# A fused sparse-attention and feed-forward kernel: a new order for the first unit, paired expert steps and casts tied to a stage

## The chip, the core and the metric

The kernel runs on one core of one Trainium2 chip. The metric is the device time of one execution in microseconds (us); before the change it is 223.5 us, the median of 9 runs (222.38 to 225.11). The engines have in-order queues of their own: TensorE (PE: matmuls into PSUM), VectorE (DVE), ScalarE (ACT), GpSimd (POOL) and SyncE (SP, which here only issues DMAs). They wait for one another by semaphores.

## What is computed

The reference takes q, k and v of shape 4 x 8 x 768 x 64 (batch, heads, sequence, head size), in float32, and two weight matrices:

```python
k_sum = k.reshape(B, H, nb, block, D).max(axis=3)      # block = 32, nb = 24
v_sum = v.reshape(B, H, nb, block, D).mean(axis=3)
scores_l = scale * q @ k.T, kept only where |i - j| < 16
scores_s = scale * q @ k_sum.T + log(block)
a = softmax over both kinds of scores together
x = a @ concat(v, v_sum)                               # heads side by side: 3072 x 512
h = x @ w_in                                           # 512 x 2048
g = h * sigmoid(1.702 * h)
out = g @ w_out                                        # 2048 x 512, out is 3072 x 512
```

Each query looks at its neighbours closer than 16 places and at 24 block summaries: the maximum of each block of keys, the mean of each block of values.

## The kernel before, in words

**Units.** The 3072 rows are cut into 8 units of 384 rows: unit `u` is half `u % 2` of batch `u // 2`. A unit's feed-forward part has an input stage and an output stage. The input stage, `ff_in`, makes 16 column tiles of `h`, each from 4 matmuls of 128 x 384 that add up over the four head pairs, and ACT applies the gate to each tile and writes it to `gT`. The output stage, `ff_out`, makes 3 row blocks of 128 rows from 16 matmuls of 128 x 512 each; ACT copies a block to `osb`, and SP sends it out. It is cut into 12 slots of 4 matmuls. In them `beside` puts the attention of the next unit, by the tables `plan`, `plan0` (for unit 1) and `plan1` (for unit 2): `s` are scores of a head pair (PE), their exponential (ACT) and a 0/1 mask product (DVE), `v` the product with the values and the division by the row sums for two head pairs, `x` a PE transpose of the result with a DVE copy, `d` the same by a DMA transpose, `t` the PE transposes of q for batch 1. The result is `xTT[0]` for head pairs 0 and 1 and `xTT[1]` for pairs 2 and 3; the next `ff_in` reads them. For units above 2, `ff_in(u, range(3))` goes through three column tiles at once, first with pairs 0 and 1 and then with pairs 2 and 3, so that the second pair can come later.

**Order by hand.** The wrapper `_Ordered` keeps each engine's instructions in program order. The order written in the code is so the order of each engine's queue, and an instruction that waits holds back all behind it on that engine.

**First unit.** Its attention is written out as a list of small steps, each naming its engine. SP loads k by halves of the sequence, q's first half, v by heads, then q's second half, all for batch 0. `cast_k`, `cast_q`: to bf16. `k_turn`, `q_turn`: transposes on PE. `k_own`, `q_copy`: copies out of PSUM. `k_max`, `k_blocks`, `k_sides`: block maxima, and the neighbour columns of the key tiles. `s_turn`, `s_exp`, `s_mask`: scores, exponential, mask. `b_turn`, `b_exp`: scores of the block maxima. `v_own`, `v_even`, `v_before`, `v_after`: casts of v into the value tiles. `v_sum`, `v_copy`: block sums. `av_near`, `av_blocks`, `v_norm`: values and division. `x_turn`: transposed result. A step is copied by `copy`, in which "dve_alone" stands for a DVE reduction over an axis of length one. `ff_first(p)` then multiplies pair `p` for the first `N0 = 2` column tiles. `warmth(8)` puts 8 wide matmuls on PE at the start, and `idle(n)` puts n small ones, without use for the result, between the steps. They write into spare columns of a PSUM tile that the steps use: `st["idle"]` names that tile.

**Loads of weights.** POOL issues eight loads with a change of type, four quarters of `w_in` and four of `w_out`, in its own queue between its casts. `load_w_in(0)` stands behind `v_own(1, 1, pool)`.

**Later batches.** The k of batch b+2 is loaded by SP in the output stage of an odd unit after slot 0 (`i == 1`), and v and q after slot 7 (`i == 8`). POOL's casts for the next batch are emitted at the beginning of an even unit, but nothing ties them to it: POOL starts on each as soon as its load has landed. `xk` (keys) and `xq` (queries, in the even unit at `i == 10`) are DMA transposes issued by SP; `halo_dmas` and `sum_dmas` fill the neighbour rows and the block rows of the value tiles. `rest_k` makes the block maxima and neighbour columns of the keys in the odd unit. PSUM has two pools: `psb` with 2 tiles of two banks and `pmm` with 4 of one bank.

Of the kernel before, what the change touches and what calls it, by code (L numbers as in the profile page):

```python
# [9 lines left out]
F32 = mybir.dt.float32  # L10
# [24 lines left out]
def kernel(  # L35
# [44 lines left out]

    raw = {}

# [15 lines left out]
    def load_q(b, p, half=None):  # L98
        if half is None:
            t = stage.tile([128, 2, NJ, D], F32, name=f"qf{p}", tag=f"qf{p}0")  # L100
            sp.dma_start(out=t.rearrange("p h j d -> p (h j) d"), in_=chunks(q, b, p))
            raw["q", p] = t
            return
        t = stage.tile([128, 2, JH, D], F32, name=f"qf{p}{half}", tag=f"qf{p}{half}")
        sp.dma_start(out=t.rearrange("p h r d -> p h (r d)"),
                     in_=q[b, 2 * p:2 * p + 2, half * HALF:(half + 1) * HALF]
                     .rearrange("h (p r) d -> p h (r d)", r=JH))
        raw["q", p, half] = t

# [205 lines left out]
    def idle(n):  # L315

        tile, o, start = st["idle"]
        for i in range(n):
            pe.matmul(out=tile[:, o:o + 120], lhsT=warm[:, 0:128], rhs=warm[:, 0:120],
                      start=start, stop=True, skip_group_check=True)  # L320

# [64 lines left out]
    def k_turn(p):  # L386
        src = cast.pop(("k", p))
        big = st["K", p] = psb.tile([128, 1024], F32, name="ps_k", tag="big")
        st["idle"] = big, 904, True
        for half in range(2):  # L390
            for r in range(JH):
                pe.matmul(out=at(big, half * 512 + r, [[JH, 128]]),
                          lhsT=src[:, half, r].rearrange("p h d -> p (h d)"),
                          rhs=ident, start=True, stop=True)
# [25 lines left out]
    def q_turn(p, half=0):  # L420
        src = cast.pop(("q", p))
        if half:
            ps = psb.tile([128, 1024], F32, name="ps_q", tag="big")
        else:
            ps = pmm.tile([128, 512], F32, name="ps_q", tag="mm")
        st["Q", p] = ps
        for r in range(JH):
            pe.matmul(out=ps[:, r * 128:r * 128 + 128],
                      lhsT=src[:, r].rearrange("p h d -> p (h d)"),
                      rhs=ident, start=True, stop=True)  # L430

    def q_copy(p, eng, half=0):

        copy(eng, qT[p][0][:, half * HALF:half * HALF + HALF].rearrange("p (c r) -> p r c", r=JH),
             st["Q", p][:, 0:HALF].rearrange("p (r c) -> p r c", r=JH))

    def s_turn(p):

        big = st["S", p] = psb.tile([128, 1024], F32, name="ps_s", tag="big")
        score_tiles(big, p, 0, 0)  # L440
        st["idle"] = big, 904, True

# [27 lines left out]
    def b_exp(g):  # L470
        ab = st["ab", g] = attp.tile([128, HALF], BF16, name="ab", tag="ab")
        act.activation(out=ab, in_=st["B", g][:, 0:HALF], func=ACT.Exp, scale=scale)

    def v_own(p, hh, eng):
# [24 lines left out]
    def v_copy(p, eng):  # L499
        for hh in range(2):  # L500
            r0 = p % 2 * 64 + hh * 32
            o = p * 128 + hh * D
            copy(eng, vs4[r0:r0 + nb, 2 * p + hh, 0:D], st["VT"][r0:r0 + nb, o:o + D])
        if p == NP - 1:
            st["idle"] = st["VT"], 0, True

# [4 lines left out]
    def av_near(p):  # L511
# [3 lines left out]
        for hh in range(2):  # L515
            for j in range(JH):
                for e in range(2):
# [4 lines left out]
                              start=(hh == 0 and j == 0), stop=False, skip_group_check=True)  # L522
        if p < 2:
            st["idle"] = st["V", p // 2], p % 2 * 512 + 392, False

# [14 lines left out]
    def x_turn(p):  # L540
        src = x_sb.pop(p)
        if p == 0:
            st["X", 0] = pmm.tile([128, 2, HALF], BF16, name="ps_x", tag="mm")
        elif p == 2:
# [121 lines left out]

    N0 = 2
    ph0, seen = [], []
# [38 lines left out]

    gate = consts.tile([128, 2], F32, name="gate")
    dve.memset(gate, 0.0)

# [12 lines left out]
    load_v(0)  # L723
    for p in range(NP):
        load_q(0, p, 1)
    hold = consts.tile([16, 16], BF16, name="hold")
# [5 lines left out]
    cast_k(act, 0, 0)  # L732
    cast_k("dve_alone", 0, 1)
    cast_k(act, 1, 1)
    cast_k(pool, 2, 1)
    cast_k(dve, 1, 0)
    k_turn(0)
    k_own(0, dve)
    cast_k(act, 2, 0)
    idle(5)  # L740
    k_turn(1)
    idle(5)
    k_turn(2)
    k_max(0)
    k_own(1, act)
    k_sides(0, dve)
    cast_k(act, 3, 0)
    k_own(2, act)
    k_blocks(0, pool)
    cast_k(dve, 3, 1)  # L750
    k_sides(1, pool)
    k_sides(2, pool)
    k_max(1)
    cast_q(pool, 2, 0)
    cast_q(act, 0, 0)
    idle(4)
    k_turn(3)
    cast_q("dve_alone", 1, 0)
    k_max(2)
    idle(2)  # L760
    q_turn(0)
    k_own(3, act)
    k_sides(3, dve)
    k_blocks(1, pool)
    q_turn(1)
    q_copy(0, act)
    cast_q(pool, 3, 0)
    q_copy(1, act)
    q_turn(2)
    k_blocks(2, pool)  # L770
    idle(3)
    b_turn(0)
    v_own(0, 0, act)
    s_turn(0)
    s_turn(1)
    v_before(0, pool)
    k_max(3)
    v_own(0, 1, "dve_alone")
    b_turn(1)
    q_copy(2, dve)  # L780
    s_exp(0)
    s_exp(1)
    v_even(0, pool)
    q_turn(3)
    b_exp(0)
    v_sum(0)
    s_mask(0, dve)
    s_mask(1, dve)
    v_own(1, 0, act)
    q_copy(3, dve)  # L790
    v_own(2, 0, "dve_alone")
    v_own(1, 1, pool)
    s_turn(2)
    idle(10)
    v_sum(1)
    load_w_in(0)
    v_own(2, 1, "dve_alone")
    s_exp(2)
    s_turn(3)
    k_blocks(3, pool)  # L800
    idle(3)
    b_turn(2)
    v_after(0, act)
    b_turn(3)
    av_near(0)
    v_copy(1, dve)
    v_before(2, pool)
    v_before(1, "dve_alone")
    v_even(2, act)
    v_sum(2)  # L810
    v_copy(0, dve)
    v_own(3, 1, "dve_alone")
    v_copy(2, dve)
    v_own(3, 0, pool)
    v_even(1, act)
    v_after(1, act)
    s_exp(3)
    load_w_in(1)
    idle(6)
    av_blocks(0, 0, D + 1)  # L820
    av_near(1)
    v_after(2, act)
    v_sum(3)
    b_exp(1)
    av_blocks(1, 0, D + 1)
    s_mask(2, dve)
    s_mask(3, dve)
    v_even(3, pool)
    av_near(2)
    v_norm(0)  # L830
    av_blocks(2, 0, D + 1)
    v_after(3, act)
    v_copy(3, act)
    v_before(3, pool)
    idle(7)
    x_turn(0)
    v_norm(1)
    av_near(3)
    av_blocks(3, 0, D + 1)
    v_norm(2)  # L840
    idle(2)
    x_turn(1)
    gelu_soon()
    copy(act, xT[0], st["X", 0 // 2][:, 0 % 2])
    copy(act, xT[1], st["X", 1 // 2][:, 1 % 2])
    idle(8)
    ff_first(0)
    idle(2)
    x_turn(2)
    v_norm(3)  # L850
    copy(dve, xT[2], st["X", 2 // 2][:, 2 % 2])
    idle(6)
    x_turn(3)
    copy(dve, xT[3], st["X", 3 // 2][:, 3 % 2])
    ff_first(1)
    ff_first(2)
    ff_first(3)
    load_w_in(2)
    load_w_in(3)
    for c in range(4):  # L860
# [8 lines left out]
    for p in range(NP):  # L869
# [6 lines left out]
    plan1 = {0: ["t0"], 1: ["t1"], 2: ["s0", "s1"], 4: ["t2"], 5: ["t3"],  # L876
             6: ["v0", "s2", "s3", "d0"], 9: ["v1"], 11: ["x1"]}

# [4 lines left out]
    def beside(u, slot):  # L883
        b, half = u // 2, u % 2
        for what in (plan0 if u == 1 else plan1 if u == 2 else plan).get(slot, ()):
# [11 lines left out]
            else:  # L897
                tx(i)

    for u in range(2 * B):  # L900
        b, half = u // 2, u % 2
        todo = {}
        if u == 0:
            for p in range(NP):
                cast_q(dve, p, 1)
                todo[4 + p] = [lambda p=p: (q_turn(p, 1), q_copy(p, dve, 1))]
        elif u == 1:
# [13 lines left out]
        elif half == 0 and b + 1 < B:  # L921
            s = (b + 1) % 2
            for p in range(NP):
                cast_k(pool, p)
                if p % 2:
                    xk(p // 2, s)
            for p in range(NP):
                cast_v(pool, s, p, 0)
                cast_v(pool, s, p, 1)
            for p in range(NP):  # L930
                cast_q(pool, p)
        elif b + 1 < B:
            s = (b + 1) % 2
            todo = {1: [lambda: rest_k(0, s)], 3: [lambda: rest_k(1, s)],
                    6: [lambda: rest_k(2, s)], 8: [lambda: rest_k(3, s)]}
        if u == 1:
            for p in range(NP):
                clear_kx(pool, p, 0)
            clear_vw(pool, 0)
        if u > 2:  # L940
            ff_in(u, range(3))
        for nt in range(0 if u else N0, NT):
            if u <= 2 or nt > 2:
                ff_in(u, (nt,))
# [10 lines left out]
        for ms, part in order:  # L955
# [16 lines left out]
            elif half and b + 2 < B and i == 1:  # L972
                for p in range(NP):
                    load_k(b + 2, p)
            elif half and b + 2 < B and i == 8:
                load_v(b + 2)
                for p in range(NP):
                    load_q(b + 2, p)
            elif half == 0 and 0 < b < B - 1 and i == 10:
                s = (b + 1) % 2  # L980
                vsum(s, range(NJ))
                block_sums()
                xq(0, s)
                xq(1, s)
                w5 = vw[s].rearrange("p (j e) h c -> p j e h c", e=2)
# [32 lines left out]
```

## Time and profile before

| | |
|---|---|
| median of 9 runs | 223.5 us (222.38 to 225.11) |
| the profiled execution: its time, its span | 222.64 us, 220.9 us |
| first expert matmul (`ph`) | 24.31 us into the span |
| first unit's output stage begins | 36.70 us |
| input stages of units 1 to 7 begin | 50.83, 78.73, 102.89, 126.34, 150.56, 173.62, 196.68 us |
| last output copied | 217.58 us |
| DMA, mean over the span | 169 GB/s |
| read from and written to HBM | 27.26 MB, 6.29 MB |

A stage begins where the chain of waits passes from one kind of expert matmul to the other. In the rows of the profile, PE is the matmuls and PEld the loading of their weights; `ph` is the PSUM tile of the input stage, `po` of the output stage, `ps_s` of scores, `ps_av` of values, `ps_k` and `ps_q` of transposed k and q. A row of a timeline has start, length, engine, line, operation, output and inputs, the shape, how many in a row, and in brackets how long the engine was idle before and who released it. As all instructions go through one wrapper, their line is 27.

### The profile page before, as it was taken

What the parts mean: (1) busy time and instruction counts of PE and PEld (TensorE: products, weight loads), DVE (VectorE), ACT (ScalarE), POOL (GpSimd) and SP (SyncE); (2) the same over time, 40 slices, a digit from 0 to 9 for tenths busy, and PEclk for the clock granted to TensorE, in tenths of its full rate; (3) what the DMA queues carried; (4) which work ended last, traced back from release to release, by engine and by line L of the source; (5) the groups of instructions that cost most, each with busy time, mean ns of one, the idle gap of its engine ahead of it and who ended that gap; (6) DMA issues with size and microseconds to landing.
All of it is one profiled execution on the core that took longest, in us unless ns stands there. A gap on an engine that the chain in (4) does not pass through costs nothing.

```text
span 220.9 us, 5025 instructions
## 1 busy us (share of the span) xinstructions
PE 209.4 (95%) x1989; PEld 118.3 (54%) x1989; DVE 92.0 (42%) x262; ACT 136.9 (62%) x241; POOL 67.2 (30%) x164
## 2 busy tenths in 40 slices
PE   7588999999999999999999999999999999999993
PEld 3456665556554556454655465445654564556542
DVE  5789780545985710376408100649026001700000
ACT  3688568465677657862788277735786478637420
POOL 5377983044954438410004166400000000000000
PEclk9999999999999999999999999999999999999999
DMA  5999999999999999999999999999703300340012
GB/s 169 315 218 235 212 211 217 165 230 214 254 314 195 224 236 218 239 148 179 173 193 235 200 225 215 204 157 217 157 14 98 119 0 3 83 131 2 0 47 96
DMA packets 94408, 37.36 MB, mean 169 GB/s; under 512 B 78705, under 2 KB 91441, under 8 KB 94385
## 3 DMA queue, kind: packets, MB, share of 16 engines
q1 hardware_dynamic: 90160, 32.85, 73.7%
q0 software_dynamic: 4224, 4.19, 11.5%
q8 instruction: 15, 0.25, 0.5%
q14 instruction: 9, 0.07, 0.1%
HBM read 27.26 MB, written 6.29 MB: 152 GB/s over the span
## 4 chain that ended last, share of the span: by engine, by line
PE 76%; DMA 8%; DVE 6%; SPq 4%; ACT 2%; issue 2%; POOL 0%; DVEq 0%; ACTq 0%; POOLq 0%
PE ph L27 36%; PE po L27 32%; DMA w_in_sb<-in_moe_w_in_dram 4%; SPq L27 4%; PE ps_av L27 3%; PE ps_s L27 2%; DMA vf<-in_v_dram 2%; DMA xT<-x 2%; DVE a_sb L27 2%; ACT a_sb L27 1%; DVE kx L27 1%; PE ps_q L27 1%; DVE ks L27 1%; DVE qT L27 1%; PE ps_vs L27 1%
## 5 line engine op out<-in xcount | busy, mean ns | idle before, releaser
L27 PE MATMUL po<-w_out_sb,gT 128*128 128x512 bf16 (+2 forms) x400 | 89.0, 371 | 0.0
L27 PE MATMUL ph<-xT,w_in_sb 128*128 128x384 bf16 x512 | 86.3, 326 | 1.0 <-DMA xT<-x 0.4
L27 ACT ACTIVATE gT<-ph 128x384 bf16<-128x384 f32 x128 | 61.6, 491 | 27.4 <-PE ph L27 27.2
L27 PEld LDWEIGHTS <-w_in_sb 128*128 128x128 bf16 x512 | 49.4, 98 | 33.8 <-issue 1.0
L27 PEld LDWEIGHTS <-gT 128*128 128x128 bf16 x400 | 36.4, 98 | 38.5
L27 DVE TENSOR_TENSOR a_sb<-a_sb,mk 128x768 bf16<-128x768 bf16 x32 | 19.4, 620 | 75.1 <-ACT a_sb L27 73.9
L27 ACT ACTIVATE osb<-po 128x512 f32<-128x512 f32 (+1 forms) x24 | 14.2, 592 | 36.8 <-PE po L27 36.7
L27 ACT ACTIVATE a_sb<-ps_s 128x768 bf16<-128x768 f32 x32 | 24.3, 806 | 7.6 <-PE ps_s L27 7.6
L27 POOL CAST vw<-vf 128x768 bf16<-128x768 f32 (+3 forms) x35 | 24.2, 720 | 14.4 <-DMA vf<-in_v_dram 13.9
L27 POOL CAST kb<-kf 128x768 bf16<-128x768 f32 (+1 forms) x13 | 11.0, 848 | 47.1 <-DMA kf<-in_k_dram 47.1
L27 ACT ACT_TABLE_LOAD x16 | 20.5, 1283 | 1.1 <-PEq L1002 0.8
L27 DVE TENSOR_TENSOR x<-ps_av,rc 128x384 bf16<-128x384 f32 x28 | 15.6, 557 | 1.0
L27 POOL CAST qb<-qf 128x384 bf16<-128x384 f32 (+1 forms) x18 | 11.4, 651 | 9.1 <-DMA qf<-in_q_dram 6.0
L27 PEld LDWEIGHTS <-a_sb 128*64 128x64 bf16 x384 | 8.1, 111 | 7.3 <-DVE a_sb L27 3.6
L27 DVE TENSOR_REDUCE ks<-kx 128x24 bf16<-128x768 bf16 x12 | 11.2, 937 | 0.3 <-ACT kx L27 0.3
L27 PE MATMUL ps_av<-vw,a_sb 128*64 128x65 bf16 x384 | 10.3, 198 | 0.6 <-DVE a_sb L27 0.4
L27 DVE COPY osb<-po 128x128 f32<-128x128 f32 x1 | 0.3, 292 | 24.9 <-PE po L27 24.9
L27 DVE COPY kx<-kx 128x80 bf16<-128x80 bf16 (+4 forms) x52 | 9.6, 237 | 0.9 <-ACT kx L27 0.9
L27 PE MATMUL ps_s<-qT,kx 64*128 64x64 bf16 x384 | 9.2, 191 | 0.5 <-DVE qT L27 0.2
L27 PEld LDWEIGHTS <-kx 64*128 64x128 bf16 x384 | 7.0, 95 | 4.8 <-issue 3.9
L27 PEld LDWEIGHTS <-warm 128*128 128x128 bf16 x71 | 5.4, 107 | 6.8 <-issue 5.2
L27 DVE RECIPROCAL rc<-ps_av 128x6 f32<-128x6 f32 x32 | 6.0, 188 | 6.6 <-PE ps_av L27 6.6
(70 smaller groups left out, 118.1 us busy)
## 6 DMA issues: line engine op xcount, KB each, us to landing
out_dram<-osb SPq DMA_DIRECT2D x23, 256.0 KB, 2.3
kf<-in_k_dram SPq DMA_DIRECT2D x12, 384.0 KB, 6.2
vf<-in_v_dram SPq DMA_DIRECT2D x12, 384.0 KB, 6.4
qf<-in_q_dram SPq DMA_DIRECT2D x16, 192.0 KB, 4.2
qf<-in_q_dram SPq DMA_DIRECT2D x8, 384.0 KB, 6.3
w_in_sb<-in_moe_w_in_dram POOLq DMA_DIRECT2D x4, 512.0 KB, 9.5
w_out_sb<-in_moe_w_out_dram POOLq DMA_DIRECT2D x4, 512.0 KB, 16.6
kf<-in_k_dram SPq DMA_DIRECT2D x8, 192.0 KB, 3.5
```

Source lines behind the costliest of these rows:

```text
L27: r = f(*a, **kw)
```

## The change

- **First unit.** The list of steps is rewritten: other orders and other engines for many steps. `load_w_in(0)` now stands behind `v_own(1, 0, pool)` and `k_sides(3, pool)`.
- `q_turn` writes its three transposes with a step of 3 in PSUM for the first half, and `q_copy` then copies a plain run.
- **Idle matmuls.** `idle` does nothing until a bank is named. It is the bank of q's last turn, once that is copied out, then that of the second block scores, once their exponential is taken. 34 idle matmuls are asked for instead of 63; each is 128 wide instead of 120.
- **Late q.** The second half of q of batch 0 is one load of all heads, issued by POOL between the third and the last quarter of `w_in`, instead of four loads by SP after v. Its turns in unit 0 come after column tiles 11 to 14, instead of 4 to 7.
- `N0` is 3: `ff_first` multiplies three column tiles.
- **Pairs.** `ff_in(u, range(3))` is used for units 1 and 2 also. For unit 2, the first two head pairs are transposed by PE (`x0` at slot 8) and no longer by DMA (`d0` at slot 6).
- **Casts.** From unit 2 on, POOL copies one element of the unit's first gate output to `gate2` before its casts, so that they can't begin earlier. k and v are cast in an even unit, q in the odd unit after it. q is loaded in the even unit after the key transposes, and `xq` is issued in the odd unit behind the casts of q. v is loaded after slot 6 instead of slot 7.

The core of the diff (in the list of the first unit only the start and the end, and the loads):

```diff
     def load_q(b, p, half=None):
...
+        if half and p == 0:
+            late[0] = stage.tile([128, NP, 2, JH, D], F32, name="qfl", tag="qfl")
+            if b == 0:
+                pool.dma_start(out=late[0].rearrange("p i h r d -> p (i h) (r d)"),
+                               in_=q[0, :, HALF:S].rearrange("h (p r) d -> p h (r d)", r=JH))
...
     def idle(n):
-        tile, o, start = st["idle"]
+        if st.get("idle") is None:
+            return
         for i in range(n):
-            pe.matmul(out=tile[:, o:o + 120], lhsT=warm[:, 0:128], rhs=warm[:, 0:120],
-                      start=start, stop=True, skip_group_check=True)
+            pe.matmul(out=st["idle"][:, 0:128], lhsT=warm[:, 0:128], rhs=warm[:, 0:128],
+                      start=True, stop=True)
...
     def q_turn(p, half=0):
-            pe.matmul(out=ps[:, r * 128:r * 128 + 128],
+            pe.matmul(out=ps[:, r * 128:r * 128 + 128] if half else at(ps, r, [[JH, 128]]),
...
     def q_copy(p, eng, half=0):
+        if half == 0:
+            copy(eng, qT[p][0][:, 0:HALF], st["Q", p][:, 0:HALF])
+            if p == NP - 1:
+                st["idle"] = st["Q", p]
+            return
...
     def b_exp(g):
+        if g:
+            st["idle"] = st["B", g]
...
-    N0 = 2
+    N0 = 3
...
     cast_k(act, 0, 0)
-    cast_k("dve_alone", 0, 1)
-    cast_k(act, 1, 1)
+    cast_k(pool, 2, 0)
+    cast_k(dve, 0, 1)
+    k_turn(0)
     cast_k(pool, 2, 1)
+    k_own(0, act)
     cast_k(dve, 1, 0)
-    k_turn(0)
-    k_own(0, dve)
-    cast_k(act, 2, 0)
+    cast_k(dve, 1, 1)
+    k_turn(1)
+    k_own(1, act)
+    cast_k(act, 3, 0)
+    k_turn(2)
+    k_own(2, act)
+    cast_q(act, 0, 0)
+    k_sides(0, pool)
+    cast_k(pool, 3, 1)
+    k_turn(3)
...
+    v_own(1, 0, pool)
+    s_mask(2, dve)
+    v_sum(0)
+    v_own(1, 1, act)
+    k_sides(3, pool)
...
+    load_w_in(0)
+    v_own(2, 0, pool)
...
+    av_blocks(3, 0, D + 1)
     ff_first(0)
+    v_norm(2)
     x_turn(2)
+    copy(act, xT[2], st["X", 2 // 2][:, 2 % 2])
     v_norm(3)
+    ff_first(1)
     x_turn(3)
     copy(dve, xT[3], st["X", 3 // 2][:, 3 % 2])
     ff_first(2)
     ff_first(3)
     load_w_in(2)
+    for p in range(NP):
+        load_q(0, p, 1)
     load_w_in(3)
...
-             6: ["v0", "s2", "s3", "d0"], 9: ["v1"], 11: ["x1"]}
+             6: ["v0", "s2", "s3"], 8: ["x0"], 9: ["v1"], 11: ["x1"]}
...
+    def pool_after(u):
+        pool.tensor_copy(out=gate2, in_=gT[u % 2][:, 0, 0:1])
+
+    def turn_keys(u, b):
+        s = b % 2
+        pool_after(u)
+        for p in range(NP):
+            cast_k(pool, p)
+            if p % 2:
+                xk(p // 2, s)
+        for p in range(NP):
+            load_q(b, p)
+        for p in range(NP):
+            cast_v(pool, s, p, 0)
+            cast_v(pool, s, p, 1)
+
+    def turn_queries(u, s):
+        pool_after(u)
+        for p in range(NP):
+            cast_q(pool, p)
+            if p % 2:
+                xq(p // 2, s)
...
-                todo[4 + p] = [lambda p=p: (q_turn(p, 1), q_copy(p, dve, 1))]
+                todo[11 + p] = [lambda p=p: (q_turn(p, 1), q_copy(p, dve, 1))]
...
         elif half == 0 and b + 1 < B:
+            todo = {0: [lambda: turn_keys(u, b + 1)]}
         elif b + 1 < B:
             s = (b + 1) % 2
-            todo = {1: [lambda: rest_k(0, s)], 3: [lambda: rest_k(1, s)],
+            todo = {0: [lambda: turn_queries(u, s)],
+                    1: [lambda: rest_k(0, s)], 3: [lambda: rest_k(1, s)],
                     6: [lambda: rest_k(2, s)], 8: [lambda: rest_k(3, s)]}
...
-        if u > 2:
+        if u:
             ff_in(u, range(3))
...
-            elif half and b + 2 < B and i == 8:
+            elif half and b + 2 < B and i == 7:
                 load_v(b + 2)
-                for p in range(NP):
-                    load_q(b + 2, p)
             elif half == 0 and 0 < b < B - 1 and i == 10:
                 s = (b + 1) % 2
                 vsum(s, range(NJ))
                 block_sums()
-                xq(0, s)
-                xq(1, s)
```

## The prediction

> **What bounds the kernel now.** I read the engine sums first, then a table of stages, the chain of waits, and single engines in order of time. Part 1 of the page says that TensorE is the bound:
>
> ```profile
> PE 209.4 (95%) x1989; PEld 118.3 (54%) x1989; DVE 92.0 (42%) x262; ACT 136.9 (62%) x241; POOL 67.2 (30%) x164
> ```
>
> Only 11.5 us of the span have no matmul. The stage table says where (columns: stretch, its length, PE busy, then PEld, DVE, ACT, POOL, clock, DMA share, GB/s):
>
> ```profile
> 5.00:10.00 5.00, 3.14 (x28) 2.70 (x27) 3.48 (x7) 2.47 (x5) 1.42 (x5) 1.00 1.05 325
> 20.00:24.30 4.30, 3.45 (x66) 2.70 (x62) 3.72 (x11) 3.25 (x8) 4.28 (x7) 1.00 1.19 234
> 25.90:36.70 10.80, 10.80 (x75) 6.61 (x74) 6.44 (x25) 7.20 (x15) 8.23 (x45) 1.00 1.22 215
> 36.70:50.80 14.10, 13.80 (x159) 7.01 (x157) 6.08 (x14) 8.28 (x12) 2.88 (x3) 1.00 1.15 201
> 89.30:102.90 13.60, 13.48 (x170) 6.41 (x168) 7.47 (x17) 7.57 (x11) 2.49 (x3) 1.00 1.11 181
> 136.80:150.50 13.70, 13.29 (x169) 6.59 (x168) 7.29 (x17) 7.55 (x11) 3.32 (x4) 1.00 1.03 192
> 184.00:196.70 12.70, 12.70 (x147) 6.27 (x145) 4.96 (x12) 7.57 (x11) 0.00 (x0) 1.00 0.29 75
> ```
>
> From 25.9 us on PE has hardly a gap: a unit's input stage is 64 matmuls in 10.4 us, its output stage 48 wide ones (10.3 us) and the next unit's attention. An undisturbed output stage lasts 12.66 us (184.02 to 196.68 in the chain), or 13.11 with the 0.45 us of block sums (ps_vs). So there are two places to gain: the start, and the excess of some stages. At the start the chain of waits (start, length, what) reads:
>
> ```profile
> 14.89 0.50 POOL vw L27
> 15.39 0.04 issue
> 15.43 8.83 DMA w_in_sb<-in_moe_w_in_dram
> 24.26 0.05 issue
> 24.31 0.50 PE ph L27 x2
> ```
>
> The first expert matmul starts when w_in's first quarter lands, and that load waits in POOL's queue for a cast of v. Two of the unit's 64 input matmuls (0.163 us each) are done when the others begin at 25.86, an effective start at 25.5. The loads that follow are close behind (issue to landing of the w_in quarters, then w_out's):
>
> ```profile
> DMA to landing us min/median/max: 8.8/9.5/11.9
> DMA to landing us min/median/max: 13.9/16.6/19.3
> ```
>
> Asked issue by issue, with the issues at 15.43, 17.97, 20.37, 21.10 and 21.84, w_in lands at 24.26, 27.4, 30.0, 33.0 and w_out's first quarter at 35.7. They are first used at 24.3, 28.1, 31.4, 34.1 and 36.7 (0.65 us a column tile, 0.17 a q turn): the last two have only 1 us of slack.
>
> **The change: first unit.** Loads of k, q, v keep their order, so their landings stand: k halves 3.46 to 8.72 (waits of the casts), q 9.5 to 11.1 (issue plus 4.6), v at 14.77, 17.5 and 19.43 for the fourth, seventh and eighth half (waits of POOL), the others set between at 0.9 us. With the rows of before (ACT 0.52 and DVE 0.36 for a half cast, 0.81 for k_own on ACT, 0.95 for k_max, 0.82 for a turn of k, 0.62 a mask, 0.76 a norm) I walked the new order through the in-order queues. Before, the fill matmuls sat in the bank being read, and the turn behind them waited:
>
> ```profile
> 7.19 0.42 PE L27 MATMUL ps_k<-warm 128*128 128x120 bf16 x5 [1.05 <-DVE kx L27]
> 8.37 0.82 PE L27 MATMUL ps_k<-ident,kb 128*128 128x128 bf16 x6
> 11.51 0.67 PE L27 MATMUL ps_q<-ident,qb 128*128 128x128 bf16 x9
> ```
>
> After: k turns start at 4.7, 6.55 (cast of the half that lands at 6.12), 7.96, 9.29, against 4.66, 7.45, 8.37, 10.75; q turns at 10.1 to 11.1; s_turn(0) at 11.6 instead of 13.54. Then v's landings rule. v_sum(0) comes at 13.5 (second half 12.8, cast 0.5). ACT takes v_own(1,1) at 14.8, v_copy(0), v_even(1) and b_exp(0), so av_blocks(0) starts at 16.6 (19.41 before) and av_near(1) at 17.7. The last half of v is cast by 19.85 on DVE and 20.45 on ACT (v_even, v_after): v_sum(3) at 19.9, v_copy(3) to 20.9, av_near(3) 21.2, av_blocks(3) to 21.9, last norm to 22.7. On POOL the load of w_in's first quarter stands behind v_own(1,0) (lands 13.8, ends 14.3) and k_sides(3) (0.6): issue 14.9 instead of 15.43. The late q loads, 0.77 MB beside it before, are now behind w_in's third quarter. Quarters follow each other in 2.6 to 3.1 us, so the first lands at 22.0: 2.3 us earlier. ff_first(0) holds x_turn(2), x_turn(3) and two xT copies behind it, 22.05 to 24.6, with 12 matmuls in place of 8: effective start 22.7, 2.8 us earlier.
>
> This gain is clipped. The stream then runs 22.0, 24.7, 27.3, late q (2.0 to 2.6 us at 0.3 to 0.38 MB/us), w_in's last quarter 32.4, w_out's first 35.1. PE would want the last quarter at 30.6 and waits 1.8 us (minus a q turn). Four column tiles of 0.65 and three q turns of 0.17 end the stage at 35.5 where it was 36.7. **First term: 1.2 to 1.4, taken as 1.3 us.** The DVE casts of late q, first in DVE's queue behind xT and keys (26.3), now wait to 29.9; behind them are only the q copies (0.8 each), wanted at 35.4 or later, and masks wanted at 37.9. POOL ends its constant masks about 1 us later, 34.6, still in time. The software load of 1024 rows has no row; the w_in issue of 512 rows takes 0.74 to 0.88, so I take 0.9 to 1.7 on POOL, hidden behind a full queue.
>
> A rule against it: the Trainium skill, "PSUM — Partial Sum Buffer", Specifications, says that any non-contiguous access pattern slows matmuls significantly, and q's turns now write with step 3. The rows agree and size it: six strided k turns take 0.82, nine plain ones 0.67, so about 0.10 against 0.057 each: 0.15 us a turn on PE. By the rule alone this is a loss of 0.6; but q_copy reads plain and falls from 0.80 to about 0.5 (k_own's 0.96 for twice the width), which stands on the way to s_turn(0). I count nothing net, as v rules afterwards (bounds −0.3 to +0.6). A second: "TensorE: Matmul & The Clock Gate", in its table for kernels, allows no PE gaps over about 3 us; from its window of 3.4 us I estimate up to 1.7 us lost at half rate. Here 63 fills become 34, none before 14.3 us. The row shows clock 1.00 at 3.14 us busy of 5; the walk has turns and scores for about 6.5 of the 9.6 us after 4.7, gaps under 0.8. So by the row nothing; the rule's 1.7 stays in the range.
>
> **Three column tiles by pairs.** In unit 1 PE waited 0.32 us for the DVE copy of the second pair (50.2 to 50.8). Three tiles give 6 matmuls, 0.98 us, on the first pair. Gain 0.3 (0 if a PSUM bank comes late). In unit 2 it waited 0.37 for the DMA transpose. That becomes 6 PE transposes (0.34) and a DVE copy (0.56) at slot 8; the gap from 78.20 to 78.73 goes. Net 0.15; bounds −0.3 (a PSUM bank more, held for 1 us) to 0.4. In unit 1 the 0.27 us wait of a k turn for DVE also goes, since with an earlier start the first key chain ends before POOL's v casts.
>
> **Casts held to input stages.** Rows where POOL's casts meet DVE:
>
> ```profile
> 92.04 0.83 POOL L27 CAST qb<-qf 128x768 bf16<-128x768 f32 x1 [1.01 <-DMA qf<-in_q_dram]
> 92.08 1.66 DVE L27 TENSOR_TENSOR a_sb<-a_sb,mk 128x768 bf16<-128x768 bf16 x2 [13.12 <-ACT a_sb L27]
> 139.52 1.91 DVE L27 TENSOR_TENSOR a_sb<-a_sb,mk 128x768 bf16<-128x768 bf16 x2 [17.41 <-ACT a_sb L27]
> ```
>
> A free pair of masks lasts 1.26. The losses are 0.40, 0.65 and, at 119.22 (1.40), 0.14; the output stages of those units are 13.57, 13.80 and 12.89 long, 0.46, 0.69 and 0.23 over their base. So the masks are the excess. After, 4 k and 8 v casts at 0.83 start at the first gelu, 1.9 us into the input stage, and end at 11.9; masks come at 13.3. Free: 1.2 us (bounds 0 to 1.4). In odd units POOL's four q casts (1.9 to 5.3) meet the key copies, which stretch from 0.36 to about 1.2 as at 54.32; DVE has until 13, so nothing. xq, behind halos and sums on SP, is issued 3.6 to 7.0 into the unit and lands 4.1 later, first needed at 10.5: covered by 2 us, each us beyond would be paid. v's loads go one slot earlier, ahead of an output that then waits some 5 us on SP (76.94 to 81.96 before); it has three buffers, so nothing. q's loads leave that place and stand behind the key transposes (a rival below).
>
> **Sum.** 1.3 + 0.3 + 0.27 + 0.15 + 1.2 = 3.2 us. The profiled execution took 222.64 (span 220.9 and 1.7 around it), the lower end of the runs; it becomes 219.4. Against the median of 223.5: 220.3.
>
> **Rivals.** *Weights don't clip* (0.16): the first load starts sooner than its issue tells, or late q passes quickly; then the first term is 2.8 and the time 218.8. For it: the stream shared with late q before. Against: the same bytes before w_in's last quarter.
> *The stream starts as before* (0.20): v's last half and the software queue set its start, so the last quarter lands at 33.0; first term 36.7 − 36.1 = 0.6, the masks give half, 0.6, and the small terms lose 0.2. 1.0 in all: 222.5, own range 221.5 to 224.4.
> *SP's queue turns slower than before* (0.20): in units 2 and 4 the key transposes now wait on POOL and have q's loads, an output and both x transposes behind them. Counted from the unit's start: first pair cast at 3.6, four transposes 6.8 (10.4), four loads 7.1 (17.5), output 1.7, x transposes 3.4: 22.6. Before they ended at 23.4 and PE did not wait. A slip beyond 0.8 us is paid in both units; it eats 3.2 at 2.4 us and passes 0.5% at 3. If transposes beside v's loads cost 3.5, 225.7.
>
> **Chances.** A measurement can tell about 0.5%, 1.1 us. The forecast (219.3 to 221.5) has 0.44. Faster: 0.44 + 0.16 + 0.05 of the second rival; same: 0.15, and 0.01 of the last; slower 0.19. The range 218.2 to 224.6 leaves out 0.04 below, 0.16 above.
>
> **To look for.** Right: the first ph matmul near 22, a PE wait on w_in near 31, mask pairs near 1.26 everywhere, output stages of 13.1 and 12.7. Wrong: clock under 1.00 in the first slices, ph waiting on DMA xT at units 3 and 5, ps_s on DMA qT, or a first ph after 23.

## The result, and the profile after

The kernel after takes **221.33 us** (median of 16 runs, 220.46 to 222.43) against 223.06 for the kernel before on the same chips (53 runs): ratio 0.9925, 95% interval 0.9906 to 0.9945. That is 1.7 us faster, inside the range and in the direction forecast, but half of the 3.2 us that the sum gave. The profiled execution took 220.88 us, its span is 219.1 us. Some executions of a kernel fall into a slower state; the ratios leave those out and the medians do not, so where the two differ the ratio counts.

The same rows as before the change, first the engine sums of the page:

```profile
PE 209.2 (95%) x1966; PEld 116.4 (53%) x1966; DVE 93.4 (43%) x261; ACT 136.7 (62%) x243; POOL 69.2 (32%) x169
```

PE's work is the same; what it does not work has gone from 11.5 to 9.9 us. The stage table (stretch, length, PE busy, then PEld, DVE, ACT, POOL, clock, DMA share, GB/s), with the edges set to this kernel's stages:

```profile
5.00:10.00 5.00, 4.12 (x26) 2.11 (x25) 3.67 (x9) 3.49 (x6) 2.89 (x8) 1.00 1.06 332
20.00:23.00 3.00, 3.00 (x62) 2.51 (x60) 1.58 (x4) 1.60 (x4) 3.00 (x4) 1.00 1.23 197
25.20:37.30 12.10, 10.38 (x73) 6.31 (x71) 7.11 (x25) 7.03 (x15) 9.29 (x48) 1.00 1.19 244
37.30:50.80 13.50, 13.50 (x159) 6.92 (x157) 5.88 (x14) 7.83 (x12) 1.65 (x2) 1.00 1.09 188
89.00:102.20 13.20, 13.20 (x169) 6.46 (x168) 6.53 (x17) 7.61 (x12) 1.17 (x2) 1.00 1.04 199
135.70:148.90 13.20, 13.20 (x170) 6.50 (x169) 6.55 (x17) 7.58 (x12) 1.21 (x2) 1.00 1.26 219
```

The output stages of units 2 and 4 are as forecast: 13.2 us and full. The first input stage (third row) has 1.7 us without a matmul where there was none. PE's row and the chain of waits show for what:

```profile
34.20 0.82 PE L27 MATMUL ph<-xT,w_in_sb 128*128 128x384 bf16 x4 [1.69 <-DMA w_in_sb<-in_moe_w_in_dram]
```

```profile
13.84 0.51 POOL vw L27
14.36 1.54 POOL kx L27 x2
15.89 0.05 issue
15.94 0.32 PE ps_s L27 x10
...
20.00 0.69 POOL w_in_sb L27
20.68 0.88 POOL qfl L27
21.57 12.59 DMA w_in_sb<-in_moe_w_in_dram
34.15 0.04 issue
34.20 0.82 PE ph L27 x4
```

The last quarter of w_in is issued at 21.57 and lands at 34.15. Stage by stage (starts of the first matmul of each kind, from PE's rows in order of time), the difference between the two profiled executions is:

| | before | after | difference |
|---|---|---|---|
| first `ph` | 24.31 | 23.03 | −1.28 |
| unit 0, input stage | 12.23 | 14.28 | +2.05 |
| unit 1, input and output stage | 13.21, 15.50 | 12.41, 15.40 | −0.90 |
| output stages of units 2, 3, 4 | 13.75, 12.89, 13.82 | 13.22, 12.66, 13.22 | −1.36 |

(Unit 0's output stage is the same to 0.01, and so are the stages from unit 5 on. The span is 0.3 us shorter than these rows add up to; that lies behind the start of the last input stage.) The first unit costs 0.77 us here, where 1.3 of gain was forecast; pairs and casts give somewhat more than was forecast.

### The profile page after: what moved, and what is told of

Read it like the earlier page. It is cut to its first block, busy times and chain, and to the rows that moved or that the text cites. A ratio compares the mean times of both kernels' runs of the same rounds, so it can differ in the third digit from the quotient of the medians.

```text
span 219.1 us, 4973 instructions
## 1 busy us (share of the span) xinstructions
PE 209.2 (95%) x1966; PEld 116.4 (53%) x1966; DVE 93.4 (43%) x261; ACT 136.7 (62%) x243; POOL 69.2 (32%) x169
## 2 busy tenths in 40 slices
DMA packets 92711, 37.15 MB, mean 170 GB/s; under 512 B 77857, under 2 KB 89569, under 8 KB 92689
## 4 chain that ended last, share of the span: by engine, by line
PE 84%; DMA 10%; POOL 2%; SPq 1%; DVE 1%; issue 0%; DVEq 0%
PE po L27 39%; PE ph L27 35%; DMA w_in_sb<-in_moe_w_in_dram 6%; PE ps_av L27 4%; PE ps_s L27 3%; DMA vf<-in_v_dram 3%; DMA kf<-in_k_dram 2%; PE ps_q L27 1%; SPq L27 1%; POOL vw L27 1%; POOL kx L27 1%; DVE qT L27 1%; PE ps_t L27 1%; PE ps_vs L27 1%; PE ps_x L27 1%; PE ps_vt L27 0%
## 5 line engine op out<-in xcount | busy, mean ns | idle before, releaser
L27 ACT ACTIVATE gT<-ph 128x384 bf16<-128x384 f32 x128 | 60.9, 491 | 26.9 <-PE ph L27 26.8
L27 DVE TENSOR_TENSOR a_sb<-a_sb,mk 128x768 bf16<-128x768 bf16 x32 | 17.6, 555 | 65.8 <-ACT a_sb L27 64.5
L27 ACT ACTIVATE osb<-po 128x512 f32<-128x512 f32 (+1 forms) x24 | 14.2, 592 | 37.0 <-PE po L27 36.8
L27 ACT ACTIVATE a_sb<-ps_s 128x768 bf16<-128x768 f32 x32 | 24.2, 805 | 6.7 <-PE ps_s L27 6.7
L27 POOL CAST vw<-vf 128x768 bf16<-128x768 f32 (+3 forms) x36 | 25.0, 749 | 3.2 <-DMA vf<-in_v_dram 2.9
L27 POOL COPY gate<-gT 128x1 bf16<-128x1 bf16 x4 | 0.8, 191 | 60.4 <-ACT gT L27 60.4
L27 DVE COPY kx<-kx 128x80 bf16<-128x80 bf16 (+4 forms) x48 | 12.6, 315 | 0.0
L27 PE MATMUL ps_av<-vw,a_sb 128*64 128x65 bf16 x384 | 9.8, 198 | 0.8 <-DVE x_sb L27 0.8
L27 DVE CAST qT<-ps_q 128x384 bf16<-128x384 f32 (+1 forms) x8 | 7.2, 900 | 4.9 <-PE ps_q L27 4.8
```

What stands on the lines that cost most here:

```text
L27: r = f(*a, **kw)
```

## Where the weights lose their lead

Issues and landings of the loads show the lead going. w_in's quarters and w_out's first land at 24.26, 27.4, 30.0, 33.0, 35.7 before, and at 21.4, 24.2, 28.7, 34.15, 37.05 after, with late q at 30.9 between. The first quarter is 2.8 us earlier, the last 1.15 later. The window from 16 to 18 us before, then the windows after (columns as above):

```profile
16.00:18.00 2.00, 1.67 (x39) 1.23 (x37) 1.97 (x5) 2.00 (x5) 1.62 (x6) 1.00 1.13 249
```

```profile
14.00:16.00 2.00, 0.86 (x10) 0.33 (x11) 1.96 (x5) 1.54 (x5) 2.00 (x4) 1.00 1.24 216
16.00:18.00 2.00, 2.00 (x43) 1.61 (x44) 1.25 (x4) 1.99 (x6) 1.94 (x4) 1.00 0.59 109
18.00:20.00 2.00, 1.23 (x27) 0.98 (x25) 1.57 (x4) 1.45 (x4) 1.90 (x5) 1.00 1.15 188
20.00:22.00 2.00, 2.00 (x40) 1.66 (x38) 1.22 (x3) 0.64 (x2) 2.00 (x3) 1.00 1.23 192
22.00:24.00 2.00, 1.69 (x30) 1.08 (x26) 1.09 (x4) 1.92 (x5) 2.00 (x4) 1.00 1.10 162
```

In 16 to 18 us the DMA engines are half empty: share 0.59, 109 GB/s, where before it was 1.13 and 249. In quarters of a microsecond the share is 0.13 to 0.20 from 17.0 to 18.0 and back at 1.08 from 18.25. SP has issued its last load of v at 14.7 us; before, four late q loads followed it and ran on beside the first weights. After, nothing follows, and the first load from POOL's queue, issued at 15.83, moves hardly a byte until 18.0. It was no quicker before: issued at 15.43, it moved its first packets at 17.9, but the late q filled the time. So the stream of weights does not start sooner; its first load has the engines for itself and lands sooner. At 24.26, when the first quarter lands before, POOL's queue has moved 0.92 MB there, nearly two quarters, and the late q is all but done: 5.70 MB since the start, against 5.13 after. From 14 to 30 us 3.53 MB moved before and 3.30 after (the dip at 22 to 24 is made up by 353 GB/s at 26 to 28): 0.23 MB less, 1.1 us at 0.21 MB/us, the lateness of the last quarter. **My theory A**: the late q load, moved to POOL's queue, leaves DMA time unused, and all that comes behind the first weights pays. Rivals: POOL's queue issues too late; the place of late q in the stream; fewer idle matmuls (clock).

## The experiments

**Late q by SP again**, the rest as after; `load_q` issues each load on SP. Ratios here and below are to the kernel before, with 95% intervals.

```diff
+    for p in range(NP):
+        load_q(0, p, 1)          # four loads by SP, behind load_v(0)
...
-    for p in range(NP):          # one load by POOL, behind load_w_in(2)
-        load_q(0, p, 1)
```

> The changed kernel with late q loaded as before, by four loads of SP right behind v. Theory A (the DMA engines ran empty for about 1.2 us between the end of v and the first weights, since nothing was queued behind v): the share of the DMA in 16 to 18 us goes from 0.59 back to over 1.1, w_in's first quarter lands later (23.5 to 24.3) but the last one at 32.3 to 33.0 instead of 34.15, PE's wait for it falls under 0.5 us, and the time is 0.6 to 1.5 us below the changed kernel. Theory B (late q in front of w_in's last quarter costs its own 2.3 us, no time is lost on the engines): the first quarter still lands by 22 and the last by 31.9, and PE doesn't wait; 1.7 us below. Theory C (the late start is what the wait hides, so a later first matmul gives all back): within 0.3 us of the changed kernel.

219.68 us (6 runs), ratio 0.9847 (0.9805 to 0.9889): 1.65 us below after. The window in question and PE's wait for w_in, from this run:

```profile
16.00:18.00 2.00, 2.00 (x42) 1.61 (x43) 1.42 (x5) 1.99 (x6) 1.94 (x4) 1.00 1.02 189
27.52 5.37 PE L27 MATMUL ph<-xT,w_in_sb 128*128 128x384 bf16 x32 [0.59 <-DMA w_in_sb<-in_moe_w_in_dram]
```

PE waits 0.6 us for w_in (its second quarter) instead of 1.7 (its last), w_in's last quarter lands at 32.66, w_out's first at 35.8, and the output stage begins at 36.00. With 12 idle matmuls instead of 3 ahead of the last scores on top of that:

> The kernel with late q by SP, with 12 idle matmuls instead of 3 in front of the scores of the fourth head pair, where PE is busy 0.84 of 2 us (14 to 16 us). Theory A: the clock keeps at 1.000 in all executions, and the median is within 0.3 us of the kernel with 3, or below where that one lost the clock. Theory B (fills delay the scores behind them): 0.3 to 0.6 us above.

219.86 us, 0.9859 (0.9814 to 0.9903), its output stage from 36.29: the same. These two are the fastest versions of the study, below both kernels. The second one limits theory A, though. Its window is nearly as empty as that of after, as SP issued the last late q only at 18.14:

```profile
16.00:18.00 2.00, 1.87 (x34) 1.31 (x34) 1.50 (x4) 1.96 (x6) 2.00 (x5) 1.00 0.67 131
```

Yet w_in's last quarter lands at 32.5, and w_out's first at 36.25, half a microsecond behind the version with the full window. So these 2 us are not the whole of what late q by SP gives.

**The first weight load earlier**, behind `v_own(0, 1, pool)`, in the kernel after and in the version above.

```diff
     v_own(0, 1, pool)
+    load_w_in(0)
...
-    load_w_in(0)
     v_own(2, 0, pool)
```

> The changed kernel with the load of w_in's first quarter issued one cast and one copy step earlier in POOL's queue, right behind the casts of the first head pair of v (about 13.4 us instead of 15.8). Theory A (the DMA engines run empty between v and the first weights): the weights start while v still loads, the share of the DMA in 16 to 18 us rises from 0.59 to over 1.0, w_in's last quarter lands at 32.6 to 33.4 instead of 34.15, PE's wait of 1.7 us halves, v's last half and with it the first expert matmul come up to 1 us later; 0.5 to 1.2 us below the changed kernel. Theory B (late q in front of the last quarter costs its own length): the whole stream moves by the 2.4 us, the last quarter lands at 31.8, the wait goes; 1.7 us below.

> Both: late q by SP behind v, and the first quarter of w_in issued at 13.4 us. Theory A: with late q behind v the engines have hardly any empty time left (shares of 1.02 to 1.26 between 14 and 22 us), so the earlier issue only lets the weights take their turns from v; the last quarter lands within 0.5 us of 32.7, v's last half later, and the time is within 0.5 us of the kernel with late q by SP alone. Theory B: the stream moves by its 2.4 us again, 0.6 us below that kernel, as its rest of wait goes.

222.44 us, 0.9973 (0.9942 to 1.0005): not below after but 1.1 above, so this expectation fell. The first issue was at 13.50 and the window 16 to 18 was full (1.21), but 20 to 22 was emptier instead (0.80): the third quarter, behind POOL's later casts of v, was issued at 22.04 instead of 19.94, and PE waited 1.1 us for w_out. The hole moved. (In 5 of the 12 executions, the profiled one among them, the mean granted clock was 0.992, too; the other 7 have a median of 222.28, so the clock alone is not the cause.) With late q by SP the same move gives 220.16, 0.9871 (0.9829 to 0.9914), within 0.5 us of the version it was made from. So an earlier first issue is not what was lacking; that it was something to move meanwhile fits both runs.

**Late q behind w_in's last quarter**, its four turns after column tile 15.

```diff
     load_w_in(2)
-    for p in range(NP):
-        load_q(0, p, 1)
     load_w_in(3)
+    for p in range(NP):
+        load_q(0, p, 1)
```

> The kernel after, with the load of late q behind w_in's last quarter instead of ahead of it, and its four turns all after column tile 15. Theory A (the first stage is late because the DMA engines run nearly empty between v's end and the first weights; all that lies behind is late by it, in whatever order): w_in's last quarter lands near 31.8 us and PE does not wait for it, but w_out's first quarter still lands near 37, and the output stage of unit 0 begins at 36.8 to 37.4 us: time 220.8 to 221.8, within 0.5 us of the kernel after. Theory B (the place of late q between the quarters costs the 1.7 us that PE waits for the last quarter): the output stage begins near 35.7, 1.2 to 1.7 us below the kernel after, 219.6 to 220.2.

221.34 us, 0.9928 (0.9901 to 0.9955): exactly after. PE no longer waits for w_in, but w_out's first quarter lands at 37.4, and late q at 34.5, with casts and copies of DVE behind it (PE waits 2.0 us for these), so that the output stage begins at 37.97, 0.6 later than w_out would have allowed. Theory A holds for the total: w_out's first quarter comes no sooner in either order, and that order chooses only who waits. The kernel may owe part of its time to the late copies, so that this run alone would not settle it.

**A tiny load first** in POOL's queue, near the start.

```diff
     masks0()
+    early = consts.tile([16, 16], BF16, name="early")
+    pool.dma_start(out=early, in_=moe_w_in[0:16, 0:16])
```

> The kernel after, with one tiny load added in POOL's queue near the start of the kernel (16 x 16 elements of w_in to a tile that nobody reads), so that the first weight load is not the first transfer of that queue. The question is to what the 2.2 us belong in which the DMA engines are half empty before w_in's first bytes. Theory A (to the first use of the queue): w_in's first quarter lands 1 to 2 us sooner than 21.4 us, DMA share from 16 to 18 us near 1.0 instead of 0.59, the last quarter near 33.0, and the time 0.8 to 1.3 us below the kernel after. Theory B (to every load of this kind[...]): landings and share as in the kernel after, time within 0.4 us of it.

220.90 us, 0.9901 (0.9870 to 0.9932), 0.4 below after by the medians and 0.5 by the ratios, which the intervals don't tell apart. The first quarter needs 5.7 us from issue to landing (5.6 after) and the last lands at 33.9 (34.15); so the delay is not the queue's first use. Theory B.

**No idle matmuls** in the first unit (all 34 left out).

```diff
-    idle(3)                      # and the eight others
     s_turn(3)
```

> The changed kernel without any of the 34 idle matmuls of the first unit (the 8 wide ones at the start stay). Theory A (the clock is cut when PE does too little for some 3 us, as in 16 to 19.5 us of one execution of the first unit alone): the granted clock falls in most executions, to a mean of 0.985 to 0.992, the first expert matmul comes 0.5 to 1.5 us later, and the time is 0 to 1.0 us above the changed kernel (the wait for the last quarter of w_in takes up the rest). Theory B (turns and scores are enough by themselves, as the prediction had it): clock 1.000 in as many executions as with them, time within 0.3 us.

221.72 us, 0.9936 (0.9909 to 0.9963). The granted clock falls to half, in all 12 executions (means over the span 0.977 to 0.992):

```profile
14.00:16.00 2.00, 0.64 (x7) 0.12 (x6) 1.96 (x6) 1.82 (x5) 2.00 (x4) 1.00 1.34 223
16.00:18.00 2.00, 1.85 (x33) 1.49 (x34) 1.40 (x5) 1.99 (x6) 1.94 (x4) 0.60 0.70 112
18.00:20.00 2.00, 1.38 (x21) 1.18 (x21) 1.55 (x4) 1.36 (x4) 1.90 (x5) 0.50 1.12 181
20.00:22.00 2.00, 2.00 (x28) 1.74 (x27) 1.22 (x3) 0.83 (x3) 2.00 (x3) 0.50 1.11 135
22.00:24.00 2.00, 1.88 (x23) 1.15 (x21) 0.90 (x3) 1.95 (x4) 2.00 (x4) 0.69 1.15 175
```

Yet the first `ph` is only 0.2 us later, less than the 0.5 to 1.5 expected, and the run 0.4 slower, which the intervals don't tell apart: PE was to wait for w_in anyway (1.9 us here). Here a half-rate clock ahead of a wait cost little.

**Each part alone**, on the kernel before: the first unit; the casts; the pairs with `x0`; the pairs without `x0`; and pairs and casts together, that is, after with the old first unit.

```diff
...
-        if u > 2:
+        if u:
             ff_in(u, range(3))           # the pairs; x0 for d0 with them, or not
...
```

> The first unit of the change with its late q, idle matmuls and three first column tiles, on the loop of before (no pairs in units 1 and 2, casts not held). Theory: the new first unit moves the first expert matmul from 24.3 to 23.0 us but gains nothing at the end of the input stage of unit 0, because w_in's last quarter lands at 34.1 instead of 33.0; the output stage begins 0.8 us later than before. So 0 to 1.0 us slower than before. Rival: the first unit is worth something by itself and the loss sits in how it meets the loop: 0.5 to 1.5 us faster than before.

> Only the casts held to input stages, with the loads of q and v and the query transposes moved as in the change, on the kernel before. Theory: the mask pairs of units 2, 3 and 4 go back to 1.26 us and their output stages lose 0.35, 0.23 and 0.58 us: 1.0 to 1.4 us faster than before. Rival: the output stages were long for the DMA traffic and not for the casts, and what the change gains there comes from somewhere else: within 0.4 us of before.

> Only the three column tiles by pairs in units 1 and 2, and PE transposes in place of the DMA transpose in unit 2, on the kernel before. Theory: the waits of 0.32 and 0.37 us at the start of units 1 and 2 go and 0.34 us of transposes comes: 0.3 to 0.6 us faster. Rival: the waits were hidden by what follows, so nothing, within 0.2 us.

> The kernel before with three column tiles by pairs in units 1 and 2, and nothing else: the first pairs of unit 2 are still transposed by DMA (d0 at slot 6). The version with x0 as well was 2.05 us below the kernel before. Theory A (the pairs do it: the second pair's copy is no longer waited for at the start of units 1 and 2): 1.0 to 2.0 us below before, unit 1's input stage about 12.3 us instead of 13.2. Theory B (x0 does it, since a DMA transpose fewer lies in SP's queue and in the DMA engines in unit 1): 0.2 to 0.8 us below before; unit 1's input stage is shorter by 0.3 to 0.9 us all the same, since x0 comes after it, and the start of unit 2 keeps its wait of about 0.4 us for the transposed pair.

> The kernel after with the first unit of before (its list of steps, its fills, four late q loads by SP behind v, N0 = 2): the pairs with x0 and the held casts on the kernel before. The question is what the rewritten first unit gives beside the two others. Theory A (by itself it costs time, as its separate run says, and the parts add up): 2.05 + 0.56 = 2.6 us below before, so 219.9 to 220.6, about 0.9 us below the kernel after; first ph at 24.3 and the output stage of unit 0 at 36.7 us. Theory B (the first unit pays only together with the others, since an earlier start takes v's later load out of the way of the transposes): 221.3 or more, no better than the kernel after.

| alone on before | us | ratio (95%) |
|---|---|---|
| first unit | 224.06 | 1.0047 (1.0016 to 1.0078) |
| casts | 222.46 | 0.9975 (0.9956 to 0.9993) |
| pairs, x0 | 221.18 | 0.9908 (0.9877 to 0.9939) |
| pairs, no x0 | 222.20 | 0.9955 (0.9927 to 0.9984) |
| pairs and casts | 220.51 | 0.9883 (0.9846 to 0.9920) |

The casts alone gave less than expected (0.6 of 1.0 to 1.4): the output stages of units 2 to 4 shrank by 1.17 us as foreseen, but the input stages of units 1 and 2 grew by 0.38 and 0.47 in the profiled execution (PE waits 0.65 us in unit 1 for a cast of v on POOL and 0.32 in unit 2 for a copy of the transposed result). The pairs alone gave far more (2.0 of 0.3 to 0.6), and without `x0` 1.0. The difference sits at the start of unit 2. In the kernel before, then in the first unit alone, PE waits there for the pair that is transposed by DMA:

```profile
78.73 2.45 PE L27 MATMUL ph<-xT,w_in_sb 128*128 128x384 bf16 x14 [0.37 <-DMA xT<-x]
```

```profile
80.56 1.64 PE L27 MATMUL ph<-xT,w_in_sb 128*128 128x384 bf16 x9 [1.86 <-DMA xT<-x]
```

And SP's queue in the pairs without `x0` says why:

```profile
67.82 5.12 SPq L27 DMA_DIRECT2D kf<-in_k_dram  x4
73.07 1.65 SPq L27 DMA_DIRECT2D out_dram<-osb  x1
74.83 1.70 SPq L27 DMA_TRANSPOSE xT<-x  x1
```

The transpose stands behind four loads of k and an output that waits. It goes out at 74.07 before, 74.83 here and 75.24 in the first unit alone; the wait grows from 0.37 to 0.93 and 1.86 us. How late SP is comes from the weights. In unit 0's output stage SP's loads for batch 1 stand behind `hold`, a load of 16 x 16 elements out of w_out's third quarter, and in every profile `hold` goes out 0.01 to 0.02 us after that quarter has landed. Before, then in the first unit alone:

```profile
40.82 0.61 SPq L27 DMA_DIRECT2D hold<-w_out_sb  x1
```

```profile
42.44 0.61 SPq L27 DMA_DIRECT2D hold<-w_out_sb  x1
```

In the pairs without `x0` it is 42.05. So the first unit alone pays for its late stream twice: its output stage begins 0.45 us later (0.8 was expected), and at unit 2 PE waits 1.5 us more than before. In the pairs without `x0`, what they save in unit 1 (its input stage takes 12.30 us instead of 13.21) is partly waited for here. With `x0` this wait is gone, and unit 1's output stage takes 15.24 us instead of 16.00. For the pairs without `x0` theory B had the wait right, which stayed and grew; the time, 1.0 us below before, lies just at the edge of theory A.

Pairs and casts with the old first unit take 220.51 us: the parts add up as its theory A said (2.05 + 0.56 = 2.6 below before), though its first output stage begins at 37.28 and not near 36.7. After against it is 1.0042, with the two half-widths combined 1.000 to 1.008: the new first unit costs between nothing and 1.9 us, and gains nothing. The starts of the first output stage in the profiles point the same way. With the old first unit (five kernels) it is 36.54, 36.17, 36.52, 37.31 and 37.28; with the new one and late q on POOL's queue (six) 37.31, 36.99, 37.67, 37.97, 37.15 and 37.69; with the new one and late q by SP (three) 36.00, 36.29 and 37.13. The means are 36.8, 37.5 and 36.5. They are single executions, and scatter by more than half a microsecond.

## Why the prediction was right, and where its size was off

**First term: the wrong one.** Forecast 1.3 us of gain, measured a loss of 0.77. The attention was walked well enough: first `ph` forecast near 22, measured at 23.03. `k_sides(3)` took 1.54 us beside two mask products of DVE instead of 0.6 (issue of the first load 15.83, not 14.9), the last scores waited for it, and `av_blocks(0)` behind them came at 17.73 instead of 16.6. The step that failed is the one on which the clip was counted, "The stream then runs 22.0, 24.7, 27.3, late q (2.0 to 2.6 us at 0.3 to 0.38 MB/us), w_in's last quarter 32.4, w_out's first 35.1". It hung every later landing on the first, at the pace of a stream that is full from the start. But the first landing does not tell how far the stream is: before, 0.92 MB of weights had moved by then, after 0.64, and no late q. Measured: 21.4, 24.2, 28.7, late q 2.2, 34.15, 37.05. The first two come sooner than the forecast, the last two 1.8 and 1.9 us after it. The first twelve column tiles end at 32.18 (48 matmuls of 0.163 back from there give an effective start of 24.35, where 22.7 was forecast), so PE wanted the last quarter only at 32.5 and waited 1.69 more. With the stream as forecast it would not have waited, and the output stage would have begun near 35.6, as the sum has it: the attention's own lateness was covered by the clip, the stream's was not. Late q by SP takes back 1.65 us: shown. That the DMA engines' empty 2 us is the cause of the lateness is worked out from the bytes, and agrees with that run and with late q behind w_in; the version with 12 idle matmuls, nearly as empty there and on time with w_in's last quarter, says that it is not the whole. How much of the 1.65 us belongs to the hole and how much to late q's place and queue stays open; a run that fills this hole with other bytes was not made.

**Clock.** The sum counted nothing "by the row", with the rule's 1.7 us in the range. In the profiled execution that held (1.00 throughout), but the row I read was one of 5 to 10 us. PE is busy for 0.86 us of 14 to 16 (2.00 before), the first idle matmul comes only at 14.76, and in 5 of 17 executions of after the mean granted clock was under 0.995; these have the same median as the other 12 (221.32 and 221.33). The Trainium skill, "TensorE: Matmul & The Clock Gate", Part 1, gives half rate after an idle window of some 3.4 us. The first unit alone shows 0.52 in 16 to 18 us and 0.62 in 18 to 20, which is 3.41 us at half rate, and no idle matmuls 6.83 us: half rate agrees, and the stretches are as long as one and two such windows. But no gap of PE came near 3 us (the longest ahead of either was 0.82), so the page's limit for gaps would have let both pass. That the DMA wait hides the lost clock agrees with no idle matmuls (0.4 us, not clear of noise) and with the equal medians.

**Pairs.** Forecast 0.3 + 0.27 + 0.15 = 0.72 us; in after the two stages of unit 1 lose 0.90. The term for unit 2, 0.15, was too small in kind: it priced a wait of 0.37 us as if it were fixed, where the transposed pair is tied to SP's queue and takes whatever PE has gained by then. Without `x0` part of the other gains is lost there: the pairs alone give 1.0 us instead of 2.0.

**Casts.** Forecast 1.2, measured 1.36 in the output stages of units 2, 3 and 4; mask pairs there are 1.15 to 1.26:

```profile
91.93 1.26 DVE L27 TENSOR_TENSOR a_sb<-a_sb,mk 128x768 bf16<-128x768 bf16 x2 [12.58 <-ACT a_sb L27]
138.61 1.26 DVE L27 TENSOR_TENSOR a_sb<-a_sb,mk 128x768 bf16<-128x768 bf16 x2 [17.20 <-ACT a_sb L27]
```

Right in mechanism, and in size for these two profiles; the casts alone were worth 0.6 us. The key copies that now meet POOL's q casts stretch to 2.38 us for three (105.28), and in this profile nothing waits for them, as said. *SP's queue turns slower* did not come true here: no `ph` waits for DMA xT at units 3 and 5, no scores for DMA qT. There was little room, though: in the profiles with the first weight load earlier and with a tiny load first, `ph` waits 0.45 and 0.17 us for DMA xT at unit 3, and in three others 0.34 to 0.68 us at unit 3 or 5, put down to DVE. *Weights don't clip* did not either: they clipped more. *The stream starts as before* (222.5) is 1.2 us off, the sum against the median (220.3) 1.0. It had one thing right: the first weights moved no sooner than before. But it expected the last quarter at its old time, 33.0, and that came at 34.15.

## What to carry over

A first load that lands sooner is not a stream that ends sooner: before moving a load off the queue that filled the time, count the bytes that the DMA engines move between the last load of that queue and the first bytes of the next. A load that looks like part of one stage can also be what another queue stands behind, as w_out's third quarter is for SP: look for such ties when a stream gets later. A wait of PE for a transfer that stands in another queue behind waiting work is not a fixed price; gains ahead of it can go into it until the tie is cut, so cut it first. And a part measured alone can pay at a place that another part of the change removes.

## What was not expected of the hardware

- The first 512 KB weight load on POOL's queue took 5.6 us from issue to landing, though the DMA engines had little else from 17 us on; the first 2.2 of it moved next to nothing. Before, its first packets came 2.4 us after the issue. With a small load ahead of it on the queue it took 5.7.
- Half-rate clock needs no long gap: PE busy for 0.64 to 0.86 us of 2, with no gap over 0.82, was followed by half rate in the first unit alone and without idle matmuls, but not in every execution of after, and in none of the six with late q by SP (0.84 of 2 us).
- Three transposes (matmuls with the identity) that write PSUM with a step of 3 take 0.50 us in their row (11.14 in after), three plain ones 0.33 (34.86).
